# Four attention layers: the first layer's split weights stay on chip, and DMAs without inputs are tied to places in their queues

## Chip, cores, metric

One core of a Trainium2 chip runs the whole program. The metric is the device time of one execution in microseconds (us); the time before is the median of three runs. Engines are named as in the profile: PE (matrix products), PEld (its weight loads), DVE, ACT, POOL, and SP, which only issues DMAs.

## What is computed

Layers A, B, A, B with the same two sets of weights, on x of 2048 rows by 512 columns, with 32 heads of 16 columns:

```
x = x + A(layernorm(x));  x = x + B(layernorm(x));  x = x + A(layernorm(x));  x = x + B(layernorm(x))
qkv = x @ wqkv;  p = softmax(q @ k^T * 16 ** -0.5);  out = (p @ v) @ wo
A: query i sees keys j with 0 <= i - j < 256;   B: every query sees every key
```

## The kernel before, in words

**Tiles.** The 2048 rows are cut into four chunks c of 512. Within a sliding layer (0 and 2) the attention of a chunk runs over eight groups qd of four heads, and each group over three steps u; "step 0.3.1" below is chunk 0, group 3, u = 1. In a step PE makes scores s (L675) from tiles kt and qt, ACT takes their exponential into e (L679), POOL zeroes what the window excludes (affine_select, L742 and L745), and two steps later PE multiplies e with the values vt into acc (L752). The full layers (1 and 3) do the same with 16 steps and no mask (L719).

**Projections as side work.** The products K, Q, V of a chunk and the output product O of a finished chunk are cut into pieces of 4 to 20 matmuls (L387) and put between the steps of the attention. Lists per chunk (`side0` for layer 0) say which works are offered. A work starts when those it names as `deps` are done by a model clock kept in Python while the program is written; PE's order is fixed as written. The other engines' orders come from a scheduler, which moves an instruction forward when nothing that it knows of holds it. Each engine then runs its list in order, and an instruction that waits holds all behind it, DMA issues on SP and POOL included.

**Split weights.** Products are made from pairs of 16-bit halves. A weight of 512x512 is loaded raw in 32 bits (tile wr, 1 MB, `load_w`), ACT makes the high half and DVE the low half (tile w, L290 and L291, `parts`), and the pair is stored to DRAM (wd, 1 MB) and loaded again before each use (`weights`, L348). Weights are named `w<type>_<s>`: type 0 is A, 1 is B; s is 0 for q, 1 for k, 2 for v, 3 for o. Before the change w0_1, w0_0 and w0_2 serve two chunks from chip (`WT` holds two uses); for chunks 2 and 3 they come back from DRAM, and w0_3 always does. B's four weights are prepared (`PR`, `prep`) while chunk 0 and chunk 1 of layer 0 run.

**Operands in DRAM.** Keys and queries are stored by SP (kw, kf, qs; L508 to L512) and loaded per group: in layer 0 by POOL (`load_win`, L705 to L708), later by SP. One row block of these arrays is constant, and `fill` (L266 to L269) writes it from tiles of ones and zeros: two fills and the first qs on SP, the others on POOL.

**Ring of eight.** Each SP issue also waits until the SP DMA eight before it is done, and so does each POOL issue for POOL's. A chunk's x goes through norm on DVE (L426, L432) and a DMA transpose (L453, issued by SP, in set-up by ACT) into xc, the moving operand of K, Q and V. Tags name rings of buffers: "vf", "xc" and "vw" hold raw weights, split weights, xc and vt in turn.

Of the kernel before, what the change touches and what calls it, by code (L numbers as in the profile page):

```python
# [2 lines left out]

# [186 lines left out]
def fast_path(ctx, tc, flag, a_x, a_wqkv, a_wo, b_wqkv, b_wo, out):  # L190
# [21 lines left out]
    WT, ST, SP, pend = {}, {}, {}, []  # L212

    clock, DONE, XNR, ONR = [0.0], {}, {}, {}

    def spent(us):
        clock[0] += us
# [41 lines left out]

    def fill(t, key, c0=0, c1=1, q=nc.gpsimd):
        r4 = lambda d0, d1: rows(t).rearrange("h (d b) (c n) -> h d b c n", b=4, n=QC)[:, d0:d1, 3]
        for c in range(c0, c1):
            if key:
                q.dma_start(r4(0, 1)[:, 0, c], ones[:H])  # L266
                q.dma_start(r4(1, DH)[:, :, c], zeros[:H, None, :].broadcast_to([H, DH - 1, QC]))
            else:
                q.dma_start(r4(1, DH)[:, :, c], ones[:H, None, :].broadcast_to([H, DH - 1, QC]))  # L269


    def load_w(ty, s, tag="vf", n="wr", behind=None):
        raw = wp.tile([P, NC, D], F32, name=f"{n}{ty}_{s}", tag=tag, bufs=VB if tag == "vw" else NQ)
        if behind is not None:
            nc.vector.tensor_copy(raw[:, 0, :1], behind)
        if s < 3:
            nc.sync.dma_start(raw, mats[ty, s].rearrange("(k p) f -> p k f", p=P))
        else:

            for u in range(2):  # L280
                for h in range(4):
                    nc.sync.dma_start(raw[32 * h + DH * u:32 * h + DH * u + DH],
                                      mats[ty, s].rearrange("(k u h d) f -> u h d k f", u=2, h=4, d=DH)[u, h])
        return raw

    def parts(ty, s, raw):

        w = wp.tile([P, NC, 2, D], F16, name=f"w{ty}_{s}", tag="vf", bufs=NQ)
        for k in range(NC):
            nc.scalar.activation(w[:, k, 0, :], raw[:, k, :], AF.Copy, scale=UP[s])  # L290
# [170 lines left out]
    def project(l, s, c, act, ht=None, first=False):  # L461


        ty, n = l % 2, f"{l}_{s}_{c}" + ("" if ht is None else f"_h{ht}")
        here = n in WT or (ty, s) in WT
        w = weights(ty, s, n, *((0, D) if ht is None else (ht * P, (ht + 1) * P)))
        yield wait(0 if here else 8)
        xc = XC[l, c]
        if s == 0:
            dst = rows(qs[ty, c])  # L470
        elif ty == 0:
            dst = rows(kw[c])
        else:
            dst = rows(kf)[:, :, c * QC:(c + 1) * QC]
        sqs, begun = {}, []
        if first:
            for t in range(NHT):
                begun.append(bank())
                for k in range(NC):
                    nc.tensor.matmul(begun[t], w[:, k, 0, t * P:(t + 1) * P], xc[:, 0, k, :], start=(k == 0), stop=False)  # L480
                    spent(MM)
        for t in range(NHT) if ht is None else (ht,):
            w0 = t * P if ht is None else 0
            if first:
                ps = begun[t]
                yield from mms(ps, [(w[:, k, a, w0:w0 + P], xc[:, b, k, :]) for a, b in TERMS[1:] for k in range(NC)], go=False)
            else:
                ps = bank()
                yield from mms(ps, [(w[:, k, a, w0:w0 + P], xc[:, b, k, :]) for k in range(NC) for a, b in TERMS], 2.2)
            settle(not sqs)  # L490
            sp = vp.tile([P, 2, QC], F16, name=f"sp{n}_{t}", tag="sp", bufs=4)
            e = 1.0 / UP[s]
            with tc.high_priority(HEAD_START):
                if act:
                    nc.scalar.activation(sp[:, 0], ps, AF.Copy, scale=e)
                else:
                    nc.vector.tensor_scalar(sp[:, 0], ps, e, None, op0=ALU.mult)  # L497
                nc.vector.scalar_tensor_tensor(sp[:, 1], ps, e, sp[:, 0], op0=ALU.mult, op1=ALU.subtract)  # L498
            sq = vp.tile([P, QC], BF16, name=f"sq{n}_{t}", tag="sq", bufs=NHT)
            if act:  # L500
                nc.scalar.activation(sq, sp[:, 0], AF.Square)
            else:
                nc.gpsimd.tensor_tensor(sq, sp[:, 0], sp[:, 0], ALU.mult)  # L503
            sqs[t] = sq

            d = dst[8 * t:8 * t + 8].rearrange("h (d b) n -> (h d) b n", b=4)
            if s:
                nc.sync.dma_start(d[:, 0:2], sp[:, 0:1].broadcast_to([P, 2, QC]))  # L508
                nc.sync.dma_start(d[:, 2], sp[:, 1])
            else:  # L510
                nc.sync.dma_start(d[:, 0:2], sp)
                nc.sync.dma_start(d[:, 2], sp[:, 0])  # L512
            yield -MM if PH["full"] else -PH["run"] * MM
        return sqs

# [212 lines left out]
    def attn_win(l, c, qd, kt, qt, a):  # L728
        first = True
        for u, tiles in enumerate(WTILES):  # L730
            tiles = [p for p in tiles if c or p[0] >= 0]
            es_ = []
            for pr in range(2):
                e = exps(f"{l}_{c}_{qd}_{u}_{pr}", kt, qt, pr,
                         [(WIN + j * P, q * P, nb * P, s * P) for j, q, nb, s in tiles])
                ev = e.rearrange("p h (m n) -> p h m n", n=P)
                edges = [(s + b, q + b - j == 2) for j, q, nb, s in tiles for b in range(nb) if q + b - j != 1]
                for b, far in edges:
                    v = ev[:, :, b, :]
                    with tc.high_priority(HEAD_START):  # L740
                        if far:
                            nc.gpsimd.affine_select(v, v, pattern=[[0, 2], [-1, P]], compare_op=ALU.is_gt,  # L742
                                                    fill=0.0, base=0, channel_multiplier=1)
                        else:
                            nc.gpsimd.affine_select(v, v, pattern=[[0, 2], [1, P]], compare_op=ALU.is_ge,  # L745
                                                    fill=0.0, base=0, channel_multiplier=-1)
                es_.append(e)

            def pv(u=u, tiles=tiles, es_=es_):
# [160 lines left out]
    def run(g):  # L910
        for _ in g:
            pass

    def later(f, *a):

        yield from f(*a)
# [49 lines left out]
        return Work(later(lambda: transpose(l, c, XN.pop((l, c), ()))), 0.0, ("T", l, c), [("N", l, c)], aside=True)  # L966

    def K(l, c, act=True):
        return Work(later(keys, l, c, act), PK, ("K", l, c), [("T", l, c), ("P", l % 2, 1), ("P", l % 2, 0)], True)

    def Q(l, c, act=True, after=()):
        k = [("K", l, i) for i in (c - 1, c) if i >= 0] if l % 2 == 0 else list(after)
# [26 lines left out]
                    [("T", l, c), ("P", l % 2, 2), *after], True)  # L999

    def OO(l, c, tail=False):
        return Work(later(wo, l, c, tail), PO, ("N", l + 1, c), [("O", l, c, NHT - 1), ("P", l % 2, 3)], True)

    def NN(c, after=()):
        def gen():
            xs = load_x(0, c)
            yield wait(8)
            for i in range(4):
                stats(0, c, i, xs[i])
# [12 lines left out]
        return Work(prep(ty, s), 0.0, ("P", ty, s), after, aside=True)  # L1022

    def SW(ty, s, after):
        return Work(store(ty, s), 0.0, None, after, aside=True)

    def CM(ty, s, after=()):
        return Work(column_maxima(ty, s), 0.0, ("C", ty, s), after, aside=True)
# [9 lines left out]
    fill(kw[0], True, q=nc.sync)  # L1038
    fill(qs[0, 0], False, q=nc.sync)
    for i in range(4):  # L1040
        stats(0, 0, i, xs[i])
    mv = ST[0, 0][1]
# [35 lines left out]

    def side0(c):
        if c == 0:  # L1080
            return [F([(kw[1], True), (qs[0, 1], False), (kw[2], True), (qs[0, 2], False)]), SW(0, 1, [("K", 0, 1)]), NN(2), T(0, 2), Q(0, 1), SW(0, 0, [("Q", 0, 1)]), PR(0, 3, [("K", 0, 1)]), VV(0, 1), SW(0, 2, [("V", 0, 1, (0, 1), 0)]), PR(1, 1, [("V", 0, 1, (0, 1), 0)]), K(0, 2), NN(3, [("T", 0, 2)])]
        if c == 1:
            return [F([(kw[3], True), (qs[0, 3], False)]), T(0, 3), Q(0, 2), PR(1, 0, [("P", 0, 3)]), K(0, 3), VV(0, 2), PR(1, 2, [("P", 1, 1)]), OO(0, 0), T(1, 0), PR(1, 3, [("P", 1, 0)])]
        if c == 2:
            return [OO(0, 1), Q(0, 3), VV(0, 3), K(1, 0), T(1, 1)]
        return [F([(kf, True, k, k + 1) for k in range(NQ)] + [(qs[1, k], False) for k in range(NQ)]), K(1, 1), VV(1, 0, True, (0,)), OO(0, 2), Q(1, 0), T(1, 2), K(1, 2)]

    def side2(c):
        if c == 0:
# [89 lines left out]
```

## Time and profile before

| | us |
|---|---|
| median of three runs (lowest, highest) | 2721.22 (2715.78, 2726.24) |
| profiled execution, its own time | 2722.56 |
| its span, first to last instruction | 2720.6 |
| PE busy in the span | 2599.0 (96%) |
| ACT busy | 2376.8 (87%) |
| POOL busy, DMA issues not counted | 592.2 (22%) |

Read by stages: set-up until about 56 us, layer 0's attention from 68 to 422, a tail of projections until 482, the full layer 1, then layers 2 and 3. In the full layers ACT and PE are both over 95% busy; in layer 0 PE is nearly full and the others are not.

### The profile page before, as it was taken

Reading aid. Unit: us, or ns where it says so; the run is one execution under the profiler, and the core shown is the slowest. Engines: PE = TensorE matmul, PEld = TensorE weight load, DVE = VectorE, ACT = ScalarE, POOL = GpSimd, SP = SyncE. Lnnn points to the kernel's source line nnn. Section 1 sums busy time; section 2 is a strip of 40 time slices with the busy share of each in tenths; the row PEclk is TensorE's granted clock in tenths of the full one; section 3 lists DMA queues with packets and bytes.
Section 4 is the critical chain, followed back from the end, with each engine's and each line's share of the span. In section 5 each row is a group of like instructions: output and inputs, shape, how many; then the busy total and the mean of one; then the engine's idle time right before and its main releaser. Section 6 shows DMA issues by size and latency. Waiting matters only on the chain.

```text
span 2720.6 us, 59477 instructions
## 1 busy us (share of the span) xinstructions
PE 2599.0 (96%) x24315; PEld 751.6 (28%) x24315; DVE 859.3 (32%) x1949; ACT 2376.8 (87%) x2683; POOL 592.2 (22%) x1263
## 2 busy tenths in 40 slices
PE   7879999999999999999999999899999999999997
PEld 3233344222222222222223333422222222222221
DVE  6545654013243113111216576311222221121111
ACT  3665663999999999999997767499999999999997
POOL 2777771000000000000005688100000000000000
PEclk9999999999999999999999999999999999999999
DMA  9986766224343223212324665523343333333331
GB/s 283 277 263 203 187 197 206 77 91 124 117 118 104 64 82 109 84 64 92 100 73 148 194 168 168 158 80 103 105 121 124 124 107 111 98 108 119 97 95 49
DMA packets 300011, 353.14 MB, mean 130 GB/s; under 512 B 114432, under 2 KB 205024, under 8 KB 293712
## 3 DMA queue, kind: packets, MB, share of 16 engines
q1 hardware_dynamic: 286992, 321.16, 39.1%
q0 software_dynamic: 8512, 27.04, 3.6%
q8 instruction: 192, 3.15, 0.5%
q10 hardware_dynamic: 4224, 1.05, 0.2%
q14 instruction: 91, 0.75, 0.1%
HBM read 236.45 MB, written 96.99 MB: 123 GB/s over the span
## 4 chain that ended last, share of the span: by engine, by line
PE 77%; ACT 7%; DVE 6%; issue 4%; DMA 4%; SPq 1%; POOL 1%; ACTq 0%; DVEq 0%; POOLq 0%
PE acc L719 30%; PE s L675 20%; PE b L387 10%; PE acc L384 10%; ACT e L679 6%; PE acc L752 5%; DMA wr<-in_B_wqkv_dram 1%; PE bs L387 1%; DVE wa L321 1%; DVE ot L647 1%; DMA wr<-in_A_wqkv_dram 1%; DMA wo<-wd 1%; DVE xh L432 1%; DVE xn L426 0%; DMA w<-wd 0%
## 5 line engine op out<-in xcount | busy, mean ns | idle before, releaser
L679 ACT ACTIVATE e<-s 128x1024 f32<-128x1024 f32 (+2 forms) x2432 | 2245.6, 1112 | 152.1 <-PE s L675 126.6
L719 PE MATMUL acc<-e,vt 128*17 128x512 f32 x8192 | 1080.1, 599 | 5.0 <-DVE ot L647 4.0
L675 PE MATMUL s<-qt,kt 64*128 64x512 f16 (+3 forms) x5504 | 769.0, 355 | 44.8 <-ACT e L679 26.2
L675 PEld LDWEIGHTS <-kt 64*128 64x128 f16 x5504 | 198.1, 94 | 786.6 <-issue 764.1
L745 POOL TENSOR_SCALAR_AFFINE_SELECT e<-e 128x256 f32<-128x256 f32 x512 | 230.7, 459 | 76.5 <-ACT e L679 75.2
L719 PEld LDWEIGHTS acc<-e,vt 128*17 128x17 f32 x8192 | 136.3, 95 | 385.6 <-issue 353.3
L647 DVE STREAM_TRANSPOSE ot<-acc 128x512 f32<-128x512 f32 x128 | 91.5, 715 | 438.4 <-PE acc L719 334.7
L742 POOL TENSOR_SCALAR_AFFINE_SELECT e<-e 128x256 f32<-128x256 f32 x448 | 196.6, 445 | 56.1 <-ACT e L679 51.3
L752 PE MATMUL acc<-e,vt 128*17 128x384 f32 (+2 forms) x2816 | 196.1, 391 | 2.7 <-POOL e L742 2.7
L663 POOL TENSOR_TENSOR oh<-o,oh 128x512 f16<-128x512 f32 x31 | 36.0, 1161 | 716.9 <-DVE oh L662 653.7
L387 PE MATMUL b<-xc,w 128*128 128x512 f16 x676 | 164.7, 386 | 15.2 <-DVE sp L498 5.9
L604 POOL TENSOR_SCALAR vt<-vt 128x16 f32<-128x16 f32 (+1 forms) x96 | 24.2, 254 | 407.1 <-DVE vt L602 288.5
L503 POOL TENSOR_TENSOR sq_h<-sp_h 128x512 bf16<-128x512 f16 x27 | 28.1, 1041 | 388.9 <-DVE sp_h L497 388.9
L384 PE MATMUL acc<-xc,w 128*32 128x512 f16 x1344 | 108.9, 379 | 2.7 <-DMA xc<-xh 1.8
L384 PE MATMUL acc<-xc,w_h 128*32 128x512 f16 x1296 | 108.5, 379 | 2.3 <-DVE km L536 2.3
L387 PEld LDWEIGHTS <-w 128*128 128x128 f16 x800 | 72.5, 99 | 135.8 <-issue 57.7
L503 POOL TENSOR_TENSOR sq<-sp 128x512 bf16<-128x512 f16 x28 | 29.1, 1041 | 367.1 <-DVE sp L497 367.1
L497 DVE TENSOR_SCALAR sp_h<-acc 128x512 f16<-128x512 f32 x27 | 18.6, 690 | 282.4 <-PE acc L384 282.4
L635 DVE SCALAR_TENSOR_TENSOR x<-acc,x 128x512 f32<-128x512 f32 x60 | 41.5, 692 | 206.1 <-PE acc L384 200.1
L497 DVE TENSOR_SCALAR sp<-acc 128x512 f16<-128x512 f32 x28 | 19.3, 688 | 271.7 <-PE acc L384 271.7
L384 PE MATMUL acc<-wo,oh 128*32 128x512 f16 x1296 | 101.3, 379 | 3.3 <-DVE m_None L548 3.3
L602 DVE COPY vt<-acc 128x256 f32<-128x256 f32 (+1 forms) x36 | 18.5, 514 | 264.7 <-PE acc L384 264.7
(142 smaller groups left out, 1688.7 us busy)
## 6 DMA issues: line engine op xcount, KB each, us to landing
kt<-kf SPq DMA_DIRECT2D x128, 512.0 KB
xd<-x SPq DMA_DIRECT2D x96, 256.0 KB
x<-xd SPq DMA_DIRECT2D x96, 256.0 KB
qt<-qs SPq DMA_DIRECT2D x96, 256.0 KB
w<-wd SPq DMA_DIRECT2D x20, 1024.0 KB
qs<-sp SPq DMA_DIRECT2D x48, 256.0 KB
wo<-wd SPq DMA_DIRECT2D x12, 1024.0 KB
wv<-wd SPq DMA_DIRECT2D x17, 512.0 KB
```

The source lines that it names most:

```text
L384: nc.tensor.matmul(ps[g:g + 32], a[:, g:g + 32], b, start=(i == 0), stop=(i == len(pairs) - 1), skip_group_check=True)
L387: nc.tensor.matmul(ps, a, b, start=(go and i == 0), stop=(i == len(pairs) - 1))
L497: nc.vector.tensor_scalar(sp[:, 0], ps, e, None, op0=ALU.mult)
L503: nc.gpsimd.tensor_tensor(sq, sp[:, 0], sp[:, 0], ALU.mult)
L635: nc.vector.scalar_tensor_tensor(xs[i], ps, 1.0 / (UP[2] * UP[3]), xs[i], op0=ALU.mult, op1=ALU.add)
L647: nc.vector.transpose(ot.rearrange("p b r -> p (b r)"), a)
L675: nc.tensor.matmul(ps[:, h, s0:s0 + wd_], kt[R * h:R * h + R, pr, kc:kc + P], qt[R * h:R * h + R, pr, qc:qc + wd_], start=True, stop=True)
L679: nc.scalar.activation(e[:, :, w0:w1], ps[:, :, w0:w1], AF.Exp, scale=SCALE)
L719: nc.tensor.matmul(a[32 * h:32 * h + DH + 1, :], V[l, qd // 4, j // 8][:, j % 8, 4 * (qd % 4) + h, :], es_[h // 2][:, h % 2, :], start=(j ...
L742: nc.gpsimd.affine_select(v, v, pattern=[[0, 2], [-1, P]], compare_op=ALU.is_gt, fill=0.0, base=0, channel_multiplier=1)
L745: nc.gpsimd.affine_select(v, v, pattern=[[0, 2], [1, P]], compare_op=ALU.is_ge, fill=0.0, base=0, channel_multiplier=-1)
L752: nc.tensor.matmul(a[32 * h:32 * h + DH + 1, q * P:(q + nb) * P], V[l, (4 * c + j) // 4][:, j % 4, 4 * qd + h, :], es_[h // 2][:, h % 2, s ...
```

## The change

- `parts` keeps every A weight on chip: w0_0 to w0_2 for all four chunks, w0_3 for two. SP loses eight loads of 1 MB in layer 0 (four of w, two of wo, two of wv). No matmul is added or dropped.
- The stores of A's pairs to DRAM (`SW`) come later, after the last use in layer 0; w0_3 is stored through `SW` too.
- B's weights are prepared from chunk 1 on instead of from chunk 0 on, each after the store that frees its buffer; their raw tiles take buffers of "xc". PR(1,3) moves to chunk 3.
- Fills, raw loads, weight stores and the x loads of `NN` get `issue_after`: they are scheduled behind the last key or query store written so far (SP) or the last affine_select (POOL).
- The first two fills move behind K(0,0)'s stores; the lists of `side0` are reordered to use the weights while they are there.

```
+    def queued(e):
+        return tc.issue_after(LAST[e]) if e in LAST else nullcontext()
...
-        if ty == 0 and s < 3:
-            WT[ty, s] = [w, w]
+        if ty == 0:
+            WT[ty, s] = [w] * (NQ if s < 3 else 2)
             SP[ty, s] = w
...
     def store(ty, s):
-        nc.sync.dma_start(wd[ty, s], SP.pop((ty, s)))
+        with queued("SP"):
+            nc.sync.dma_start(wd[ty, s], SP.pop((ty, s)))
...
-        raw = load_w(ty, s)
+        raw = load_w(ty, s, "xc" if ty else "vw")
...
-                nc.sync.dma_start(d[:, 2], sp[:, 1])
+                last = nc.sync.dma_start(d[:, 2], sp[:, 1])
...
+            LAST["SP"] = last.ins
...
+                    LAST["POOL"] = last.ins
...
-        ... ("K", l, c), [("T", l, c), ("P", l % 2, 1), ("P", l % 2, 0)], True)
+        ... ("K", l, c), [("T", l, c), ("P", l % 2, 1)], True)
...
     xs = load_x(0, 1)
     run(keys(0, 0, True, None, True))
+    fill(kw[0], True, e="SP")
+    fill(qs[0, 0], False, e="SP")
```

The lists of `side0` by chunk, without the waits that the works name:

```
-  c0: F(kw1, qs1, kw2, qs2), SW(0,1), NN(2), T(0,2), Q(0,1), SW(0,0), PR(0,3), VV(0,1), SW(0,2), PR(1,1), K(0,2), NN(3)
+  c0: F(kw1, qs1, kw2, qs2), NN(2), T(0,2), Q(0,1), PR(0,3), VV(0,1), K(0,2), NN(3)
-  c1: F(kw3, qs3), T(0,3), Q(0,2), PR(1,0), K(0,3), VV(0,2), PR(1,2), OO(0,0), T(1,0), PR(1,3)
+  c1: F(kw3, qs3), T(0,3), SW(0,3), Q(0,2), VV(0,2), K(0,3), SW(0,1), PR(1,1), OO(0,0), T(1,0)
-  c2: OO(0,1), Q(0,3), VV(0,3), K(1,0), T(1,1)
+  c2: Q(0,3), SW(0,0), PR(1,0), VV(0,3), SW(0,2), PR(1,2), OO(0,1), K(1,0), T(1,1)
-  c3: F(kf, qs of B), K(1,1), VV(1,0), OO(0,2), Q(1,0), T(1,2), K(1,2)
+  c3: F(kf, qs of B), K(1,1), VV(1,0), OO(0,2), PR(1,3), Q(1,0), T(1,2), K(1,2)
```

From layer 1 on, PE and SP stand in the same order in both programs; all that moves lies before. Three places matter, with names that keep their numbers (`wr1_1` is the raw k weight of B, `e0_0_5_2_1` the exponential of layer 0, step 0.5.2, second pair).

SP, before the change, at chunk 0: a 1 MB store, two raw loads of B and a reload stand between the key stores of K(0,2).

```order
L300 DMA wd0_2_107<-w0_2_449 128x4096
L277 DMA wr1_1_1234<-in_B_wqkv_dram 128x4x512
L508 DMA kw2_94<-sp0_1_2_0_1310 128x2x512
L509 DMA kw2_94<-sp0_1_2_0_1310 128x512
L348 DMA w0_0_2_1627<-wd0_0_105 128x4096
L277 DMA wr1_0_1635<-in_B_wqkv_dram 128x4x512
L508 DMA kw2_94<-sp0_1_2_1_1411 128x2x512
```

SP after the change, first raw load of B, in chunk 1, behind K(0,3)'s last key store; below it the second and third, in chunk 2.

```order
L517 DMA kw3_95<-sp0_1_3_3_2417 128x2x512
L518 DMA kw3_95<-sp0_1_3_3_2417 128x512
L309 DMA wd0_1_106<-w0_1_203 128x4096
L285 DMA wr1_1_2458<-in_B_wqkv_dram 128x4x512
L628 DMA xd_113<-x0_0_2221 128x512
```

```order
L309 DMA wd0_0_105<-w0_0_303 128x4096
L520 DMA qs0_3_100<-sp0_0_3_3_3018 128x1024
L285 DMA wr1_0_3059<-in_B_wqkv_dram 128x4x512
L309 DMA wd0_2_107<-w0_2_449 128x4096
L564 DMA qs0_3_100<-m0_3_None_3134 8x512 x4
L285 DMA wr1_2_3653<-in_B_wqkv_dram 128x4x512
```

The raw loads leave chunk 0 and stand directly behind a 1 MB store each.

ACT, the split of wr1_1: before, in step 0.5.2.

```order
L679 ACTIVATE e0_0_5_2_1_1337<-s0_0_5_2_1_1332 128x1024
L290 ACTIVATE w1_1_1484<-wr1_1_1234 128x512 x4
L679 ACTIVATE e0_0_6_0_0_1382<-s0_0_6_0_0_1379 128x2x384
L679 ACTIVATE e0_0_6_0_1_1389<-s0_0_6_0_1_1386 128x2x384
L495 ACTIVATE sp0_1_2_1_1411<-b34_1317 128x512
```

And after the change, in step 1.6.2; the key stores ahead of its load are those of step 1.5.2.

```order
L689 ACTIVATE e0_1_6_2_0_2538<-s0_1_6_2_0_2533 128x1024
L689 ACTIVATE e0_1_6_2_1_2548<-s0_1_6_2_1_2543 128x1024
L298 ACTIVATE w1_1_2729<-wr1_1_2458 128x512 x4
L689 ACTIVATE e0_1_7_0_0_2583<-s0_1_7_0_0_2578 128x1024
L689 ACTIVATE e0_1_7_0_1_2593<-s0_1_7_0_1_2588 128x1024
```

The split still stands between exponentials, one chunk later.

POOL, the loads for group 4 of chunk 0: before, the key load stands in step 0.2.0, and a fill behind it.

```order
L706 DMA kt0_0_4_1023<-kw0_92 128x2x512
L745 AFFINE_SELECT e0_0_2_0_1_890<-e0_0_2_0_1_890 128x2x128
L742 AFFINE_SELECT e0_0_2_0_1_890<-e0_0_2_0_1_890 128x2x128
L266 DMA kf_96<-ones_85 32x512
L267 DMA kf_96<-zeros_89 32x15x512
```

After the change both loads stand behind the masks of step 0.3.1.

```order
L755 AFFINE_SELECT e0_0_3_1_0_1050<-e0_0_3_1_0_1050 128x2x128
L755 AFFINE_SELECT e0_0_3_1_1_1056<-e0_0_3_1_1_1056 128x2x128
L614 TENSOR_SCALAR vt0_1_0_0_923<-vt0_1_0_0_923 128x32
L715 DMA qt0_0_4_1022<-qs0_0_97 128x2x512
L716 DMA kt0_0_4_1021<-kw0_92 128x2x512
```

The load moved from six steps ahead of its first use, step 0.4.0, to two. The loads of group 5 stand likewise behind step 0.4.1, and those of group 6 in chunk 3 behind step 3.5.1 (before: behind 3.3.1 and 3.3.2).

More of the change, by code (lines that the diff above doesn't have):

```diff
@@ L1 @@
 from collections import deque
-from contextlib import ExitStack
+from contextlib import ExitStack, nullcontext
 import concourse.bass as bass
@@ L214, in fast_path @@
     clock, DONE, XNR, ONR = [0.0], {}, {}, {}
+    LAST = {}
+    def queued(e):
+        return tc.issue_after(LAST[e]) if e in LAST else nullcontext()
     def spent(us):
@@ L258, in fast_path, with fill @@
     nc.vector.memset(lsum, 0.0)
-    def fill(t, key, c0=0, c1=1, q=nc.gpsimd):
+    def fill(t, key, c0=0, c1=1, e="POOL"):
+        q = nc.gpsimd if e == "POOL" else nc.sync
         r4 = lambda d0, d1: rows(t).rearrange("h (d b) (c n) -> h d b c n", b=4, n=QC)[:, d0:d1, 3]
-        for c in range(c0, c1):
+        with queued(e):
+          for c in range(c0, c1):
             if key:
@@ L275, in load_w @@
             nc.vector.tensor_copy(raw[:, 0, :1], behind)
[L276 to L283, printed above, removed]
+        with queued("SP"):
+            if s < 3:
+                nc.sync.dma_start(raw, mats[ty, s].rearrange("(k p) f -> p k f", p=P))
+            else:
+                for u in range(2):
+                    for h in range(4):
+                        nc.sync.dma_start(raw[32 * h + DH * u:32 * h + DH * u + DH],
+                                          mats[ty, s].rearrange("(k u h d) f -> u h d k f", u=2, h=4, d=DH)[u, h])
         return raw
@@ L299, in store @@
     def store(ty, s):
-        nc.sync.dma_start(wd[ty, s], SP.pop((ty, s)))
+        with queued("SP"):
+            nc.sync.dma_start(wd[ty, s], SP.pop((ty, s)))
         yield 0.0
     def prep(ty, s):
-        raw = load_w(ty, s)
+        raw = load_w(ty, s, "xc" if ty else "vw")
         yield wait(20)
@@ L508, in project @@
                 nc.sync.dma_start(d[:, 0:2], sp[:, 0:1].broadcast_to([P, 2, QC]))
-                nc.sync.dma_start(d[:, 2], sp[:, 1])
+                last = nc.sync.dma_start(d[:, 2], sp[:, 1])
             else:
                 nc.sync.dma_start(d[:, 0:2], sp)
-                nc.sync.dma_start(d[:, 2], sp[:, 0])
+                last = nc.sync.dma_start(d[:, 2], sp[:, 0])
+            LAST["SP"] = last.ins
             yield -MM if PH["full"] else -PH["run"] * MM
@@ L968, in K @@
     def K(l, c, act=True):
-        return Work(later(keys, l, c, act), PK, ("K", l, c), [("T", l, c), ("P", l % 2, 1), ("P", l % 2, 0)], True)
+        return Work(later(keys, l, c, act), PK, ("K", l, c), [("T", l, c), ("P", l % 2, 1)], True)
     def Q(l, c, act=True, after=()):
@@ L1001, in OO @@
     def OO(l, c, tail=False):
-        return Work(later(wo, l, c, tail), PO, ("N", l + 1, c), [("O", l, c, NHT - 1), ("P", l % 2, 3)], True)
+        return Work(later(wo, l, c, tail), PO, ("N", l + 1, c), [("O", l, c, NHT - 1), ("P", l % 2, 3)] + [("S", 0, 3)] * (l == 0 and c > 1), True)
     def NN(c, after=()):
         def gen():
-            xs = load_x(0, c)
+            with queued("SP"):
+                xs = load_x(0, c)
             yield wait(8)
@@ L1024, in SW @@
     def SW(ty, s, after):
-        return Work(store(ty, s), 0.0, None, after, aside=True)
+        return Work(store(ty, s), 0.0, ("S", ty, s), after, aside=True)
     def CM(ty, s, after=()):
@@ L1037, in fast_path @@
     raw = {m: load_w(0, m, "xc") for m in (1, 0, 2)}
-    fill(kw[0], True, q=nc.sync)
-    fill(qs[0, 0], False, q=nc.sync)
     for i in range(4):
@@ L1080, in side0 @@
         if c == 0:
[L1081 removed]
+            return [F([(kw[1], True), (qs[0, 1], False), (kw[2], True), (qs[0, 2], False)]), NN(2), T(0, 2), Q(0, 1), PR(0, 3, [("K", 0, 1)]), VV(0, 1), K(0, 2), NN(3, [("T", 0, 2)])]
         if c == 1:
[L1083 removed]
+            return [F([(kw[3], True), (qs[0, 3], False)]), T(0, 3), SW(0, 3, [("P", 0, 3)]), Q(0, 2), VV(0, 2), K(0, 3), SW(0, 1, [("K", 0, 3)]), PR(1, 1, [("S", 0, 1)]), OO(0, 0), T(1, 0)]
         if c == 2:
[L1085 to L1086 removed]
+            return [Q(0, 3), SW(0, 0, [("Q", 0, 3)]), PR(1, 0, [("S", 0, 0)]), VV(0, 3), SW(0, 2, [("V", 0, 3, (0, 1), 0)]), PR(1, 2, [("S", 0, 2), ("P", 1, 0)]), OO(0, 1), K(1, 0), T(1, 1)]
+        return [F([(kf, True, k, k + 1) for k in range(NQ)] + [(qs[1, k], False) for k in range(NQ)]), K(1, 1), VV(1, 0, True, (0,)), OO(0, 2), PR(1, 3, [("P", 1, 2)]), Q(1, 0), T(1, 2), K(1, 2)]
     def side2(c):
```

4 lines of the change are left out of this document (2 added, 2 removed).

## The prediction, made before the changed kernel ran

> **What bounds the kernel now.** First the stages: busy time of each engine by stretch of the span, with granted PE clock, share of the DMA engines and GB/s in the last three columns.
>
> ```profile
> core 0: us, PE busy (x) PEld busy (x) DVE busy (x) ACT busy (x) POOL busy (x), PEclk, DMA share, GB/s
> 0.00:56.00 56.00, 36.70 (x169) 17.37 (x170) 37.10 (x89) 21.67 (x37) 12.75 (x31) 0.97 0.95 287
> 56.00:108.00 52.00, 51.31 (x366) 18.68 (x365) 30.41 (x73) 34.83 (x53) 35.02 (x76) 0.97 0.92 243
> 108.00:168.00 60.00, 37.27 (x319) 12.59 (x317) 36.18 (x83) 33.74 (x49) 39.28 (x78) 0.83 0.99 312
> 168.00:240.00 72.00, 71.09 (x653) 28.54 (x646) 31.55 (x73) 50.21 (x64) 56.69 (x129) 1.00 0.66 217
> 240.00:250.00 10.00, 5.51 (x36) 1.86 (x34) 9.41 (x26) 2.69 (x3) 5.74 (x14) 0.85 0.68 220
> 335.00:422.00 87.00, 85.28 (x810) 36.70 (x812) 46.78 (x110) 58.67 (x74) 64.72 (x148) 1.00 0.64 191
> 482.00:2720.00 2238.00, 2174.78 (x20883) 575.00 (x20879) 589.48 (x1332) 2098.83 (x2302) 306.88 (x626) 0.99 0.36 108
> ```
>
> From 482 on, 82% of the span, nothing that the change moves stands in PE's or SP's order, so I leave that part at its length and expect it to begin earlier or later as a block. In layer 0 PE sets the pace (71.1 of 72 us busy in 168 to 240) except in one stretch: from 108 to 168 it is idle for 60 - 37.3 = 22.7 us and runs at a clock of 0.83, with the DMA engines full (0.99). So layer 0 is PE work plus stalls, and the question is which stalls go. PE's waits up to 482, with total, times and longest:
>
> ```profile
> PE s L675 <- ACT e L679: 16.2, 8, 10.6
> PE b L387 <- DVE sp L498: 6.8, 4, 5.3
> PE acc L752 <- POOL e L742: 2.7, 2, 2.1
> PE b L387 <- issue: 2.3, 1, 2.3
> ```
>
> The first two lie almost all in chunk 0. Why, ACT and SP show in order of time (start, duration, and in brackets the idle time before and what ended it):
>
> ```profile
> 127.66 2.19 ACT L290 ACTIVATE w<-wr 128x512 f16<-128x512 f32 x4 [8.27 <-DMA wr<-in_B_wqkv_dram]
> 159.07 1.15 ACT L290 ACTIVATE w<-wr 128x512 f16<-128x512 f32 x2 [8.54 <-DMA wr<-in_B_wqkv_dram]
> ```
>
> ```profile
> 111.96 0.49 SPq L277 DMA_DIRECT2D wr<-in_B_wqkv_dram  x1
> 116.82 0.38 SPq L508 DMA_DIRECT2D kw<-sp  x1
> 126.61 0.34 SPq L509 DMA_DIRECT2D kw<-sp  x1
> ```
>
> ACT stands 8.3 and 8.5 us before a split of B's raw weights, with exponentials behind it; and between two halves of one key store SP stands 9.8 us, with the sp buffers that PE's next product needs. The chain of waits has the two loads (start, length):
>
> ```profile
> 111.96 15.67 DMA wr<-in_B_wqkv_dram
> 145.50 13.55 DMA wr<-in_B_wqkv_dram
> 240.89 5.95 DMA w<-wd
> ```
>
> A megabyte takes 14 to 16 us there and 6 us where the DMA share is 0.68.
>
> **What goes, in order of time.** Rows of PE around the other stalls, a usual row of four matmuls, and DVE's wait for x at the start:
>
> ```profile
> 55.82 4.47 PE L387 MATMUL bs<-xc,w 128*128 128x512 f16 x12 [5.35 <-DVE st L406]
> 60.12 2.75 PE L387 MATMUL b<-xc,w 128*128 128x512 f16 x12
> 126.63 1.87 PE L387 MATMUL b<-xc,w 128*128 128x512 f16 x4 [5.33 <-DVE sp L498]
> 161.18 0.61 PE L675 MATMUL s<-qt,kt 64*128 64x128 f16 x4 [10.59 <-ACT e L679]
> 246.88 3.46 PE L387 MATMUL b<-xc,w 128*128 128x512 f16 x8 [4.49 <-DMA w<-wd]
> 71.04 1.04 PE L387 MATMUL b<-xc,w 128*128 128x512 f16 x4
> ```
>
> ```profile
> 7.85 0.69 DVE L406 BATCH_NORM_STATS2 st<-x 128x6 f32<-128x512 f32 x1 [0.83 <-DMA x<-in_A_x_dram]
> ```
>
> (a) Start: six fills of POOL and three of SP no longer share the DMA engines with the first x tiles, whose last wait was 0.83 us: 1 us, between 0 and 1.6.
> (b) K(0,1) waits 5.35 us at 50.5 for transposed x, then runs its first twelve matmuls in 4.47 instead of 2.75 us. What is late is the four transposes on ACT's queue, issued under a DMA share of 0.95. They now come before the last evictions of Q(0,0), with 3 MB of fills and a 1 MB store less around them. 7.1 us go; ACT must wait in between for DVE's xh, which I put at 2 us on PE: 5 net, between 0 and 7.
> (c) K(0,2) waits 2.3 us at 108.6 for xc and a reload of w0_1; the reload and two stores ahead of it are gone: 2.3 (0 to 2.3).
> (d) The stretch 108 to 168: 22.7 - 2.3 = 20.4 us idle, and slow matmuls (four in 1.87 us where 1.04 is usual, and so on). A clock of 0.83 over 37.3 us of work bounds the latter at 6.3; I take 4. No raw load, no reload and one 1 MB store is left in chunk 0: 24 (12 to 26).
> (e) The reload of w0_0 for Q(0,3): 4.49, and eight matmuls in 3.46 where twice 1.04 is usual: 6 (4.5 to 6).
> (f) POOL's wait for chunk 3's queries, stored late, goes as Q(0,3) moves ahead of O: 2.7 (0 to 2.7).
> Sum: 1 + 5 + 2.3 + 24 + 6 + 2.7 = 41.
>
> **What comes.** (g) *Late key loads.* POOL in order of time, PE's scores, and the landing of POOL's loads (KB, median us):
>
> ```profile
> 97.26 0.79 POOL L705 DMA_DIRECT2D qt<-qs  x1
> 98.06 0.77 POOL L745 TENSOR_SCALAR_AFFINE_SELECT e<-e 128x256 f32<-128x256 f32 x2
> ```
>
> ```profile
> 101.12 0.56 PE L675 MATMUL s<-qt,kt 64*128 64x384 f16 x4
> 106.29 0.61 PE L675 MATMUL s<-qt,kt 64*128 64x384 f16 x8
> ```
>
> ```profile
> kt<-kw POOLq DMA_DIRECT2D x32, 256.0 KB, 4.5
> kw<-zeros POOLq DMA_DIRECT2D x3, 480.0 KB, 9.6
> ```
>
> The row at 98.06 is the two masks of step 0.3.1; without the load ahead of them they end at 98.0. Then qt and kt go out at 98.0 and 98.8, and kt lands 4.5 later, at 103.3, where the scores of 0.4.0 stood at 101.12: 2.2 us of wait. Group 5 stands behind the masks of 0.4.1, which end near 106; kt lands at 106 + 0.8 + 4.5 = 111.3, where 0.5.0 would follow the scores at 106.29 by some 2.5: 2.5 of wait. Group 6 of chunk 3 stands nearer its use too; with DMA engines at 0.64 there, a few tenths. I take 5 in all: between 0 (landings 2.5 us shorter) and 25 (these three and group 7 of chunk 3 land like the fills in 9.6, each 5.1 later: 5 + 4 x 5.1).
>
> (h) *Raw loads of B in chunks 1 and 2.* Side work of chunk 1 takes 3.4 to 4.2 us a step (starts of scores):
>
> ```profile
> 213.03 0.61 PE L675 MATMUL s<-qt,kt 64*128 64x256 f16 x8
> 217.25 0.61 PE L675 MATMUL s<-qt,kt 64*128 64x384 f16 x8
> 220.62 0.61 PE L675 MATMUL s<-qt,kt 64*128 64x128 f16 x8
> ```
>
> In the new order of ACT some ten exponentials' worth of time, three steps, lies between K(0,3)'s last matmul and the split of wr1_1: 4.2 + 3.7 + 2.4 = 10.3 us, of which 2.3 pass until SP issues the load, so 8.0 are left for the 1 MB store ahead of it and the load. 2 MB take 6.7 us at the 312 GB/s of the full stretch, or 2 x 5.95 = 11.9 by the reload of (e): a wait between 0 and 3.9. The other two (wr1_0 and wr1_2) stand the same way. I take 1 each, nearer the quick end since the share was 0.66 there before: 3, between 0 and 25 (three waits of the 8.3 to 8.5 of before).
>
> The Trainium skill, "DMA: Bandwidth & Descriptors", section "Queues, rings and completion order", has each DMA engine take a ring's descriptors in ring order, and one issuer's DMAs share a ring; so a raw load would begin only behind the store. The same page's table of measured sizes has 6.15 us for 1 MB, by which (h) were three times 4.3, 13 in place of 3. The reload's 5.95 agrees with that figure; that the store holds the load up no row of before shows.
>
> (i) *Steps without side work.* In the new order of PE six steps of chunk 0 and chunk 3 have no side work; before the change there were six too, but four of them lay at the stall of 108 that goes. PE then waits for ACT:
>
> ```profile
> 403.22 0.39 PE L675 MATMUL s<-qt,kt 64*128 64x256 f16 x4 [1.04 <-ACT e L679]
> ```
>
> Half of 1.04 at each: 3 (0 to 6).
>
> (j) *Twelve fills on POOL in chunk 3*, tied between masks. One issue, and POOL's waits in 330 to 422 (total, times, longest):
>
> ```profile
> 79.62 0.70 POOL L267 DMA_DIRECT2D kf<-zeros  x1
> ```
>
> ```profile
> POOL e L742 <- ACT e L679: 10.6, 13, 2.0
> POOL qt L705 <- PE s L675: 6.5, 5, 1.9
> ```
>
> 12 x 0.70 = 8.4 us go into 17.1 us of waits in these two rows; the masks are two steps ahead of PE's product. I take 2: 0 to 8.4.
>
> At nothing I put these. K no longer waits for q's preparation, and the two fills moved behind K(0,0) stand on SP ahead of nothing that PE uses before step 0.0.0; if they hold up the loads of group 0, that is three issues, 3 x 0.7 by POOL's row. Raw tiles of B use buffers of "xc", which are held until an earlier chunk's products are done; the load then waits in SP with the x loads behind it, and a free buffer is there since T(1,0) comes after. Uncovered, that is one step of 4.2. The three late stores of A's pairs are needed only in layer 2.
>
> Sum of costs: 5 + 3 + 3 + 2 = 13. **Net 41 - 13 = 28** from the profiled execution's 2722.6 gives 2694.6. That execution stands 1.3 above the median of the three, so the forecast is 2693.
>
> **Rivals.**
> *Late loads are slow loads (same).* If all four late key loads land in 9.6 us, (g) is 25: 28 - 20 = 8 gained, 2713. For it: fills and stores still share chunk 0's engines. Against it: 4.5 is the median under a full share. It decides from landings of about 7 us.
> *ACT behind queued raw loads (slower).* Place: the three splits of wr1_1, wr1_0 and wr1_2. Each load is issued directly behind a 1 MB store. If both run at the pace of the stretch 108 to 168, the load lands 2 x 15.67 = 31.3 us after the pair's issue; with 8.0 us of cover ACT waits 23.3, three times 70, and PE's exponentials stand behind it. 70 in place of 3 is 67 more: 28 - 67 = -39, about 2760. The net turns negative once each of the three waits exceeds (28 + 3) / 3 = 10.3 us, a landing 18.3 after the issue. For it: the order puts a store ahead of each load, and ACT waited 8.3 and 8.5 before. Against it: the DMA share in 168 to 240 and 335 to 422 is 0.66 and 0.64, and eight other megabytes have gone.
> *The change does not empty the engines.* A share of 0.99 in 108 to 168 may be owed to x loads, transposes and key stores, which all stay; then half of (d) remains: 28 - 12 = 16, 2705.
>
> **How the numbers follow.** Forecast 0.62, 2676 to 2707; late loads 0.14; ACT behind raw loads 0.15; engines not emptied 0.09. The low end is all gains at their upper bounds (1.6 + 7 + 2.3 + 26 + 6 + 2.7 = 45.6) with no cost, 2722.6 - 45.6 = 2677, less the 1.3; the high end of the forecast has (g) to (j) twice as large. The range reaches to 2730: that takes in the late loads, the engines not emptied, and waits behind raw loads of up to 13 us each (31 - 39 = -8); that rival at its own price is left out. Half a per cent, 13.6 us, is about what a measurement of this kernel can tell from no change, so "same" is 2707.6 to 2734.8. Faster is the forecast and half of the engines not emptied: 0.67; slower is the raw-load rival: 0.15; same is the rest, 0.18.
>
> **What the changed profile would show.** (b) the wait of PE at the start of K(0,1) under 2 us; (d) the stretch 108 to 168 with over 55 us of PE busy and a clock near 1.00, and no ACT row waiting for wr in chunk 0; (e) no PE wait on w from wd before 300; (g) PE's scores waiting for kt on POOL's loads, 2 us twice; (h) ACT's splits of B in chunks 1 and 2 with idle time ahead under 2 us; (j) no second product of PE waiting long for masks in chunk 3. The block behind 482 keeps its 2238 us. It would be wrong if that block grew, if the raw loads' waits in (h) exceeded 10 us, or if PE in chunk 0 stayed idle for a reason other than these DMAs.

## The result, and the profile after

The changed kernel takes 2717.99 us (median of 12 runs, 2710.82 to 2722.34) where the kernel before takes 2720.36 beside it (12 runs): a ratio of 0.9987, 95% interval 0.9975 to 0.9999. The forecast was 2693, a gain of 28; the gain is 2.4. In profiled executions it is 1.0 us (2722.56 to 2721.54). Single runs of one kernel lie up to 12 us apart, so sums of profiled waits below are good to a few us, and ratios carry the verdicts; they leave out a few executions at a granted clock of 0.65 to 0.85, which took 2916 us or more.

The stages of the changed kernel, in the columns and stretches of the table before:

```profile
0.00:56.00 56.00, 38.19 (x172) 18.05 (x173) 35.07 (x87) 21.86 (x37) 6.82 (x20) 0.94 0.77 203
56.00:108.00 52.00, 48.17 (x358) 17.63 (x357) 30.59 (x73) 33.92 (x53) 31.31 (x70) 1.00 0.78 204
108.00:168.00 60.00, 54.92 (x487) 19.74 (x486) 38.36 (x91) 42.05 (x56) 52.68 (x111) 0.97 0.77 223
335.00:422.00 87.00, 74.71 (x692) 33.89 (x689) 45.61 (x105) 48.01 (x63) 53.96 (x122) 0.94 0.81 224
482.00:2720.00 2238.00, 2174.64 (x20863) 576.62 (x20859) 589.23 (x1332) 2093.98 (x2297) 306.70 (x626) 0.99 0.36 108
```

The stretch 108 to 168 did what was forecast: PE is busy 54.9 us instead of 37.3, at a clock of 0.97 instead of 0.83. But the stretch 335 to 422, where chunk 3 stands before the change, lost much of what chunk 0 won: 74.7 us busy where it was 85.3, with the DMA share up from 0.64 to 0.81. PE's waits up to 482, with total, times and longest:

```profile
PE s L685 <- DMA kt<-kw: 16.1, 6, 4.7
PE b L396 <- DVE sp L507: 9.0, 5, 3.3
PE bs L530 <- ACT sq L510: 6.9, 1, 6.9
PE s L685 <- ACT e L689: 6.4, 10, 1.1
```

The wait for ACT's exponentials has fallen from 16.2 to 6.4, and two waits are new: 16.1 us for keys and 6.9 for an eviction at the start.

Where the lead goes is read from a mark that both programs have 128 times: DVE's transpose of a finished group of heads. Here are those of group 2 of chunk 0, group 4 of chunk 1, the last groups of chunks 2 and 3, layer 1's first group and the program's last group, of before:

```profile
97.14 0.72 DVE L647 STREAM_TRANSPOSE ot<-acc 128x512 f32<-128x512 f32 x1 [1.05 <-PE acc L752]
214.69 0.72 DVE L647 STREAM_TRANSPOSE ot<-acc 128x512 f32<-128x512 f32 x1 [4.03 <-PE acc L752]
338.10 0.72 DVE L647 STREAM_TRANSPOSE ot<-acc 128x512 f32<-128x512 f32 x1 [0.83 <-PE acc L752]
423.73 0.72 DVE L647 STREAM_TRANSPOSE ot<-acc 128x512 f32<-128x512 f32 x1 [0.56 <-PE acc L752]
515.88 0.72 DVE L647 STREAM_TRANSPOSE ot<-acc 128x512 f32<-128x512 f32 x1 [3.19 <-PE acc L719]
2706.16 0.72 DVE L647 STREAM_TRANSPOSE ot<-acc 128x512 f32<-128x512 f32 x1 [10.68 <-PE acc L719]
```

And of the changed kernel:

```profile
97.01 0.72 DVE L657 STREAM_TRANSPOSE ot<-acc 128x512 f32<-128x512 f32 x1 [0.89 <-PE acc L763]
195.02 0.72 DVE L657 STREAM_TRANSPOSE ot<-acc 128x512 f32<-128x512 f32 x1 [3.60 <-PE acc L763]
316.28 0.72 DVE L657 STREAM_TRANSPOSE ot<-acc 128x512 f32<-128x512 f32 x1 [3.12 <-PE acc L763]
418.50 0.72 DVE L657 STREAM_TRANSPOSE ot<-acc 128x512 f32<-128x512 f32 x1 [0.56 <-PE acc L763]
510.90 0.72 DVE L657 STREAM_TRANSPOSE ot<-acc 128x512 f32<-128x512 f32 x1 [3.19 <-PE acc L729]
2702.94 0.72 DVE L657 STREAM_TRANSPOSE ot<-acc 128x512 f32<-128x512 f32 x1 [10.68 <-PE acc L729]
```

The differences are the lead: 0.1, 19.7, 21.8, 5.2, 5.0 and 3.2 us. Chunk 3 alone takes back 16.6. (A mark stands behind a group of heads, not behind a fixed amount of projection work; where the two programs differ in that, it is said below.) The next experiments ask why, and whether the start and the ties matter; the "lead" in them is always this difference to the kernel before.

### The profile page after: what moved, and what is told of

It is laid out like the page before. It is cut to its first block, busy times and chain, and to the rows that moved or that the text cites. A ratio compares the mean times of both kernels' runs of the same rounds, so it can differ in the third digit from the quotient of the medians.

```text
span 2719.8 us, 59481 instructions
## 1 busy us (share of the span) xinstructions
PE 2602.8 (96%) x24315; PEld 754.1 (28%) x24315; DVE 859.0 (32%) x1949; ACT 2378.3 (87%) x2683; POOL 588.2 (22%) x1263
## 4 chain that ended last, share of the span: by engine, by line
PE 75%; DVE 8%; ACT 7%; issue 4%; DMA 4%; POOL 1%; SPq 0%; ACTq 0%; DVEq 0%; POOLq 0%
PE acc L729 30%; PE s L685 20%; PE acc L393 10%; PE b L396 9%; ACT e L689 6%; PE acc L763 4%; PE bs L396 1%; DMA kt<-kw 1%; DVE ot L657 1%; DVE wa L330 1%; DVE xh L441 1%; DMA wr<-in_B_wqkv_dram 1%; DVE xn L435 1%; DMA wo<-wd 1%; DVE xh L435 0%
## 5 line engine op out<-in xcount | busy, mean ns | idle before, releaser
L685 PE MATMUL s<-qt,kt 64*128 64x512 f16 (+3 forms) x5504 | 771.0, 356 | 49.9 <-DMA kt<-kw 16.1
```

Source lines behind the costliest of these rows:

```text
L685: nc.tensor.matmul(ps[:, h, s0:s0 + wd_], kt[R * h:R * h + R, pr, kc:kc + P], qt[R * h:R * h + R, pr, qc:qc + wd_], start=True, stop=True)
```

## Experiments

All ratios are to the kernel before, run beside; the changed kernel's own is 0.9987.

**Fills of B away from chunk 3, to the end of layer 0** (bfills_tail).

```
-  c3: F(kf, qs of B), K(1,1), VV(1,0), OO(0,2), PR(1,3), Q(1,0), T(1,2), K(1,2)
+  c3: K(1,1), VV(1,0), OO(0,2), PR(1,3), Q(1,0), T(1,2), K(1,2), F(kf, qs of B) once Q(1,0) is done
```

> The changed kernel with the twelve fills of B's arrays (kf, qs of layer 1) moved behind Q(1,0), to the end of layer 0; nothing else moved. Theory: chunk 3 gives back 16.6 us (the lead falls from 21.8 us at the end of chunk 2 to 5.2 at the end of chunk 3) because these fills push POOL's key loads one to three steps back; PE waits 11.8 us for kt there. Then the waits for kt in chunk 3 vanish, the lead at the end of chunk 3 is 19 to 22 us, and the time is 12 to 16 us below the changed kernel, about 2703, unless layer 1 waits longer for kf at its start (2.6 us now). Rival: what crowds chunk 3 is the raw output weight of B (eight loads), its store and the x stores; the key loads stay late, PE still waits 8 us or more for kt in chunk 3, and the time stays within 4 us of 2718.

Measured: 2722.36 us, 0.9994 (0.9980 to 1.0008). PE's waits from chunk 3 to the start of layer 1:

```profile
PE b L396 <- DMA wo<-wd: 5.1, 1, 5.1
PE s L685 <- DMA kt<-kf: 3.9, 1, 3.9
PE s L685 <- ACT e L689: 3.4, 6, 1.0
PE b L396 <- DVE sp L507: 2.8, 1, 2.8
```

No wait for kt from kw is left in chunk 3, so the fills did cause it, as the theory said and the rival denied. Yet the time did not fall. The lead is 13.3 us at the end of chunk 3 and 5.8 at the end of layer 1's first group: the fills now run beside the load of the output weight, which lands in 12.2 us (7.3 in the changed kernel). PE waits 5.1 us for it, and the first twelve matmuls behind it take 5.13 us where 2.76 is usual. The theory's time was wrong because it took the end of layer 0 for free ground.

**The key loads ahead of the fills** (loads_first). The fills stay in chunk 3; only POOL's order changes.

```
-        q.dma_start(qt, qs[0, c]...); q.dma_start(kt..., kw[c]...); if c: q.dma_start(kt..., kw[c - 1]...)
+        with tc.high_priority(HEAD_START) if l == 0 else nullcontext():
+            q.dma_start(qt, qs[0, c]...); q.dma_start(kt..., kw[c]...); if c: q.dma_start(kt..., kw[c - 1]...)
```

> The changed kernel with POOL's key and query loads of layer 0 given priority in the scheduler; the fills stay in chunk 3. In chunk 0 the key loads of groups 4 and 5 go out two to three steps earlier, in chunk 3 those of groups 3, 5, 6 and 7 half a step to two steps earlier. Theory that the place of the load decides: the two waits of chunk 0 (4.4 us) go and of the 11.8 us in chunk 3 some 5 to 8 go: 9 to 12 us below the changed kernel, about 2707. Rival that the fills' traffic decides (a key load took 5.3 to 7.6 us to land in chunk 3, 4.5 before): the waits in chunk 0 go, those in chunk 3 stay above 8 us, and the time falls by 3 to 5 us, about 2714.

Measured: 2709.45 us, 0.9946 (0.9929 to 0.9963), that is 0.41% or 11 us below the changed kernel. Landing times of POOL's loads in chunk 3 (KB, median us), before the change, after it, and here:

```profile
kt<-kw POOLq DMA_DIRECT2D x5, 256.0 KB, 3.3
```

```profile
kt<-kw POOLq DMA_DIRECT2D x4, 256.0 KB, 6.3
```

```profile
kt<-kw POOLq DMA_DIRECT2D x4, 256.0 KB, 6.0
```

In the stretch of these rows, 338 to 424, the loads land about as slowly as in the changed kernel; over the whole of chunk 3 the median is 5.0 instead of 6.1 us. PE waits for no kt from kw in the whole layer, since the loads go out earlier: an earlier place in POOL's order is a cure. That does not make the slow landing harmless. The four loads that PE waited for in the changed kernel, second halves of 128 KB, took 5.3 to 7.6 us. At 3.8, their median before the change, the four waits would come to 1.4 us instead of 11.8, an estimate from the two traces.

**The four transposes of set-up on SP** (tr_sp).

```
-        transposed(0, 1, i, xh, nc.scalar)
+        transposed(0, 1, i, xh)
```

> The changed kernel with the four transposes of chunk 1's normalised x in set-up issued by SP in place of ACT. Theory: ACT's wait at these transposes holds the evictions of Q(0,0), which is PE's 6.9 us wait at 39; it goes, the first scores of step 0.0.0 start 4 to 6 us before 65.8, and the time falls by 4 to 6 us, about 2713. Rival: the transposes now hold SP, with the query stores of Q(0,0) behind them, so the first query loads of POOL (at 54 now) or the transposed x itself are late and the first scores start within 2 us of 65.8: no gain beyond 2 us.

Measured: 2712.90 us, 0.9962 (0.9944 to 0.9980), 0.25% or 7 us below the changed kernel. In the changed kernel ACT's rows of the start read:

```profile
36.46 5.09 ACTq L462 DMA_TRANSPOSE xc<-xh  x1
41.67 0.60 ACT L504 ACTIVATE sp<-bs 128x512 f16<-128x512 f32 x1 [4.61 <-issue]
41.69 3.55 ACTq L462 DMA_TRANSPOSE xc<-xh  x1
45.29 0.63 ACT L510 ACTIVATE sq<-sp 128x512 bf16<-128x512 f16 x1 [3.02 <-issue]
```

These two transposes occupy ACT's queue for 5.1 and 3.6 us, with evictions of Q(0,0) behind them, and PE waits for the last one. In the second of them ACT is not waiting for its input: DVE writes the last xh by 37.6, and this transpose, the fourth, starts at 41.7 and still takes 3.6 us.

```profile
36.92 0.69 DVE L441 TENSOR_TENSOR xh<-xn,xh 128x512 f16<-128x512 f32 x1
```

On SP the wait is gone, and the first scores stand at 58.0:

```profile
57.98 0.50 PE L685 MATMUL s<-qt,kt 64*128 64x384 f16 x4
```

They stood at 65.80 in the changed kernel. The rival, that SP would be held instead, does not show.

**No fill tied** (fills_free).

```
-        with queued(e):
+        with nullcontext():
```

> The changed kernel with no fill tied: POOL's fills go back to the front of its list and into chunk 0, B's twelve included, and the key loads of chunk 3 go back to their places of before. The raw loads, stores and kept weights stay as changed. Theory: chunk 3's 16 us come back and chunk 0 pays 5 to 8 us for 8 MB of fills, so the time is 8 to 11 us below the changed kernel, about 2708; the stretch 108 to 168 keeps over 50 us of PE busy. Rival: the fills' absence from chunk 0, not that of raw loads and reloads, is what gave the 25 us there; then PE is busy under 45 us in that stretch and the time is above 2718.

Measured: 2709.23 us, 0.9947 (0.9930 to 0.9964), 0.40% or 11 us below the changed kernel. The stretch 108 to 168 and chunk 3:

```profile
108.00:168.00 60.00, 56.15 (x512) 20.72 (x504) 42.71 (x97) 43.27 (x57) 54.35 (x116) 1.00 0.80 236
335.00:422.00 87.00, 82.45 (x737) 39.38 (x736) 51.81 (x114) 46.99 (x63) 47.63 (x113) 1.00 0.68 198
```

With all fills back at the front and in chunk 0, PE is as busy there as in the changed kernel. From mark to mark chunk 3 takes back 5.7 us of the lead instead of 16.6. With the raw loads and reloads gone, chunk 0 does not need the fills to go as well: the ties of the fills cost 11 us and buy nothing. The theory's time came true, its terms did not: chunk 3 gives back 10.9 us and not 16, and chunk 0 does not pay 5 to 8, since the lead at group 4 of chunk 1 is 21.3 us, above the changed kernel's 19.7.

**The tie on POOL alone, in the kernel before** (before_tied; `queued` and the place of the last mask are as in the change).

```
+        with queued("POOL") if q is nc.gpsimd else nullcontext():
         for c in range(c0, c1):
```

> The kernel before the change with POOL's fills tied behind the last mask written, as in the change, and nothing else. Theory: the tie alone costs: key loads of chunk 3 move back by one to four steps (groups 4 to 7) and PE waits 8 to 16 us for kt there; chunk 0 gains at most 5 us at the start and in the stretch 108 to 168 stays below 42 us of PE busy; 4 to 10 us slower than the kernel before, ratio 1.0015 to 1.004. Rival: the fills were what filled the DMA engines in chunk 0; PE's busy time in 108 to 168 rises by 8 us or more and the ratio is 0.998 or less.

Measured: 2731.12 us, 1.0031 (1.0016 to 1.0045): slower, as the theory said. Chunk 3's waits:

```profile
PE s L681 <- DMA kt<-kw: 13.4, 4, 6.6
```

Here the place alone is enough. The key loads of the last two groups, issued at 391.6 and 407.3, land in 4.6 and 5.0 us, and PE waits 5.7 and 6.6 us for them.

But the theory's chunk 0 was too low: PE is busy 49.0 us in 108 to 168, not under 42, and the lead is 11.3 us at the end of chunk 2 before chunk 3 takes it and 5.6 more. So here, with the raw loads still there, taking the fills out of chunk 0 does help.

**B's preparation moved, nothing else** (raw_late, then raw_late_tied).

```
-  c0: ... PR(1,1), ...   c1: ... PR(1,0), ... PR(1,2), ... PR(1,3)
+  c1: ... K(0,3), VV(0,2), PR(1,1), ...   c2: ... Q(0,3), PR(1,0), VV(0,3), PR(1,2), ...   c3: ... PR(1,3), ...
```

> The kernel before the change with one part of the change alone: the preparation of B's four weights moves from chunks 0 and 1 to chunks 1, 2 and 3. Fills stay at the front, A's weights are stored and loaded again as before. Theory: ACT's waits for the raw loads (8.3 and 8.5 us) and the key store held behind one are most of the idle time in the stretch 108 to 168, so this part alone gives 12 to 17 of the 24 us there and the time falls by 10 to 15 us against the kernel before (ratio 0.9945 to 0.996). Rival: the reloads and stores of A's weights, which stay, fill the DMA engines as well; the stretch keeps under 47 us of PE busy and the ratio stays above 0.998.

Measured: 2731.98 us, 1.0039 (1.0025 to 1.0054). The move did not happen, as SP's rows show:

```profile
138.61 0.57 SPq L277 DMA_DIRECT2D wr<-in_B_wqkv_dram  x1
142.32 0.61 SPq L277 DMA_DIRECT2D wr<-in_B_wqkv_dram  x1
152.00 1.63 SPq L277 DMA_DIRECT2D wr<-in_B_wqkv_dram  x1
```

A load without inputs goes wherever its buffer comes free in the scheduler's order, whatever list names it: all three are still in chunk 0 (before the change at 112, 128 and 146 us). Neither theory is tested by it. The second try adds the tie (`queued` as in the change):

```
+        with queued("SP") if ty else nullcontext():
```

> The kernel before the change with B's preparation moved to chunks 1 to 3 and its raw loads tied behind the last key or query store on SP, as in the change; fills, stores and reloads of A's weights stay. (In the try without the tie the scheduler had put the raw loads back into chunk 0, at 138 to 152 us.) Theory: ACT's two waits of 8 us in chunk 0 vanish, PE is busy 48 us or more in 108 to 168 and the ratio to the kernel before is 0.994 to 0.997. Rival: stores and reloads of A's weights alone keep the DMA engines full; PE's busy time there stays below 45 us and the ratio is 0.998 or above.

Measured: 2726.55 us, 1.0017 (1.0004 to 1.0030). In chunk 0 the theory holds: PE is busy 51.4 us in 108 to 168, and the lead is 13.5 us at the first group of chunk 1. Then chunk 2 takes it all. PE and ACT there:

```profile
234.80 0.61 PE L393 MATMUL b<-xc,w 128*128 128x512 f16 x1 [5.85 <-DMA w<-wd]
292.48 0.62 PE L527 MATMUL b<-sq,hsum 128*32 128x512 bf16 x4 [8.56 <-ACT vt L607]
```

```profile
291.31 0.63 ACT L296 ACTIVATE w<-wr 128x512 f16<-128x512 f32 x1 [9.28 <-DMA wr<-in_B_wqkv_dram]
```

The reload wait stays, and ACT waits 9.3 us for a raw load tied late, with an eviction behind it. So the time is the rival's (0.998 or above), but not for the rival's reason. Moving the raw loads pays only as long as no one needs them at once.

**No tie at all, weights kept** (untied).

```
-        return tc.issue_after(LAST[e]) if e in LAST else nullcontext()
+        return nullcontext()
```

> The changed kernel without any tie, on POOL or SP: A's weights stay on chip, but the scheduler puts their four stores and the first raw load of B, 5 MB, ahead of the key stores of K(0,2), and the fills at the front. Theory: SP's queue then holds K(0,2) as before the change; PE is busy under 48 us in 108 to 168 and the time is 0.998 to 1.004 of the kernel before, so the tie on SP is what the gain in chunk 0 hangs on. Rival: leaving out eight reloads is enough; PE is busy 53 us or more there and the ratio is 0.994 to 0.996, as with ties on SP alone.

Measured: 2712.45 us, 0.9958 (0.9943 to 0.9973).

```profile
108.00:168.00 60.00, 52.92 (x475) 19.20 (x474) 38.18 (x86) 40.70 (x54) 48.48 (x104) 0.97 0.82 250
```

That is the rival's time and, within 0.1 us, its busy share: chunk 0 runs even with three stores and a raw load ahead of K(0,2)'s key stores and a fourth store between them. The theory that the gain hangs on SP's tie falls. But the reloads are not all that is gone: two of the three raw loads that stood in chunk 0 before the change stand at 231 and 243 us here, without a tie, so no run leaves out the reloads alone. Against fills_free, which keeps SP's other ties (0.9947), the intervals overlap.

**Both repairs together** (trsp_free: transposes on SP, no fill tied; trsp_loads: transposes on SP, key loads first).

> The changed kernel with SP issuing the four transposes of set-up and with no fill tied, together. If the two gains lie in different places (start; chunks 0 and 3) they add: 0.25% and 0.40% below the changed kernel's 0.9987, so a ratio of 0.992 to 0.9925 to the kernel before, about 2700. Rival: a lead won before the projections at the end of layer 0 is taken back there by loads of weights that do not start earlier; then it stays at 0.9945 or above.

Measured: 2702.40 us, 0.9924 (0.9907 to 0.9941): the gains add.

> The changed kernel with SP issuing the four transposes of set-up, and with POOL's key and query loads of layer 0 given priority, the fills staying tied. By the same sum as for the kernel without ties: 0.25% and 0.41% below 0.9987, so 0.992, about 2700, with no wait of PE for kt above 1 us in layer 0. Rival: with an earlier start the loads of chunk 3 come into the fills' traffic and PE waits for kt again by 4 us or more; then 0.9945 or above.

Measured: 2701.85 us, 0.9918 (0.9901 to 0.9935), the lowest found, about 22 us below the kernel before, though its interval overlaps that of trsp_free. Its waits are read from a second run:

> The kernel with transposes on SP and loads first once more, for a profile at the usual clock. If the place of the key loads decides, PE waits for kt under 1 us in all of layer 0 and layer 1's first group ends 20 to 24 us before that of the kernel before; if the earlier start brings the loads into the fills' traffic, PE waits for kt by 4 us or more in chunk 3.

Measured: 2699.46 us beside 2723.64, one run each. PE's largest waits up to 482, apart from the first for x:

```profile
PE b L396 <- DVE sp L507: 11.5, 7, 3.3
PE s L685 <- ACT e L689: 7.3, 11, 1.0
PE s L685 <- DMA kt<-kf: 3.1, 1, 3.1
```

No wait for kt from kw is among them. The first group of layer 1 ends at 488.0, 27.9 us ahead of before, which is more than the 20 to 24 expected. The largest wait left is for sp, which DVE writes.

## Why the prediction was wrong, point by point

Most of the gain that is missing was lost in chunk 3, 16.6 us where 2 to 4 were priced, and at the start, 5.9 of 6.

**The block from 482 on** was taken to keep its length. Its lead goes from 5.0 to 3.2 us over 2190 us, and to 0.8 at the last instruction, where the last matmuls run slower (three in 1.48 us where 0.81 is usual). That is within the spread of single runs.

**(a) and (b), the start: 6 forecast, 2.2 measured at the first scores (67.99 to 65.80), and 0.1 by group 2.** K(0,1)'s wait of 5.35 us went, as forecast. The step that failed is the 2 us put on ACT's wait for DVE's xh at the transposes: PE waits 6.9 us there, and what holds ACT at last is a transpose whose input is ready (tr_sp). The rest went in two waits of PE for sp in chunk 0 (1.54 and 1.19 us): SP issues the eight raw loads of w0_3 in one piece ahead of Q(0,1)'s first store, 7.3 us after its tile was ready (70.4); that this held the later tiles was not tried.

```profile
69.97 7.29 SPq L290 DMA_DIRECT2D wr<-in_A_wo_dram  x8
77.68 0.34 SPq L520 DMA_DIRECT2D qs<-sp  x1
```

**(c) and (d), the stretch to 168: 26.3 forecast.** The lead grows by 19.5 from group 2 of chunk 0 to group 4 of chunk 1, with 4.4 us of waits for keys in between, so some 24. This was right in size, but the parts do not add. With the raw loads out and the reloads in (raw_late_tied) the lead at group 4 of chunk 1 is 13.3 us; with the reloads and two raw loads out (untied) it is 20.6. The fills count in chunk 0 beside raw loads (before_tied) and not without them (fills_free).

**(e), (f) and (h), the rest of chunks 1 and 2: 5.7 forecast net, 2.1 measured.** Even these 2.1 are no gain: twelve matmuls of projections, 2.3 us, stand in chunk 3 now instead. No reload is waited for, the wait of (f) has fallen from 2.7 to 0.3 us, and ACT's waits for raw loads are 1.26 and 2.31 us where 1 each was taken:

```profile
202.44 9.17 DMA wr<-in_B_wqkv_dram
246.12 9.55 DMA wr<-in_B_wqkv_dram
```

A raw load behind a 1 MB store lands in 9.2 to 9.6 us, so the rival that ACT would stand behind such loads did not come. The Trainium skill's page "DMA: Bandwidth & Descriptors" has ring order (section "Queues, rings and completion order") and 6.15 us for a megabyte (section "Bandwidth"), from which the prediction estimated 12.3 us for the pair. Counted from the store's issue the load landed after 9.7 and 10.6 us, so that estimate was high here. What was missing in the forecast is three waits of PE for sp, 1.89, 1.10 and 3.31 us, in the steps beside K(0,3) and K(1,0). That DVE is late there because splits, norm and evictions crowd on it was not tried.

**(i), steps without side work: 3 forecast, none measured.** PE's waits for exponentials in layer 0, other than the one of 10.6, were 5.6 us and are 4.7.

**(g) and (j), the late loads: this step failed.** For chunk 0 it stands: 2.2 and 2.5 us forecast, 0.92 and 3.46 measured. For chunk 3 the prediction had "a few tenths" for group 6 and 2 us for the fills, and the lead fell by 16.6. The four waits for kt are these:

```profile
349.35 1.04 PE L685 MATMUL s<-qt,kt 64*128 64x128 f16 x8 [3.23 <-DMA kt<-kw]
374.59 0.71 PE L685 MATMUL s<-qt,kt 64*128 64x128 f16 x6 [4.69 <-DMA kt<-kw]
388.71 0.61 PE L685 MATMUL s<-qt,kt 64*128 64x128 f16 x8 [1.69 <-DMA kt<-kw]
400.91 0.61 PE L685 MATMUL s<-qt,kt 64*128 64x128 f16 x8 [2.15 <-DMA kt<-kw]
```

That is 11.8 us for groups 3, 5, 6 and 7, and slow matmuls behind them (eight in 1.04 where 0.61 is usual). From mark to mark, the 16.6 us are 10.9 of more idle time (12.6 instead of 1.7), the 2.3 of moved matmuls, and 3.3 of slow ones: PE is busy 89.6 us with the work that takes 86.2 in fills_free, where the clock is 1.00.

Two things were overlooked. The fills were priced as POOL's issue time (8.4 us into 17.1 of waits), while what they moved was the order behind them: four groups' loads, not one. And the landing was priced at 4.5, which the prediction calls the median under a full share; it is the median over all of layer 0, and the eight loads of 56 to 168 had 5.2. In chunk 3 the fills (4 MB), the raw output weight and its store (1 MB each) raise what is moved from 16 to 22 MB and the landing from 3.3 to 6.3 us; without fills there (fills_free) the landing is 3.8.

Of the rivals, "late loads are slow loads" (2713, with a chance of 0.14 and a price of 20) came nearest to what happened. It had half of the cause: slow landings. The other half is the place: the fills also put back the loads of groups 3 and 5 of chunk 3, which the prediction does not name. loads_first shows that an earlier place ends the waits, and before_tied that a late place makes them even at landings of 4.6 and 5.0 us.

## What to carry to other kernels

A transfer that is taken out of a full stretch and tied elsewhere is paid again by what stands behind its new place: price the orders of the loads it pushes back, not only its issue. Look at the queue of the engine that issues it, and at who waits there two steps later. And where several transfers fill a stretch together, taking out some of them may end most of the stall, so that removing the rest as well brings little: here keeping the weights, with no tie at all, brought 0.42%, and the changed kernel with all its ties 0.13%.

## What the runs showed that was not expected

The DMA transposes of set-up occupy the queue that issues them: 1.7, 2.3, 5.1 and 3.6 us for the four on ACT, 8.1 us for the same four on SP. The fourth one's 3.6 us on ACT hold no wait for its input, which was ready 4 us before; for the others the runs do not tell how much is waiting for DVE's xh. Twelve fills of constants at the end of layer 0 were slow among themselves: the four of 480 KB for the queries, issued in 2.6 us, had a median of 13.6 us to landing, against 7.1 when they stood one by one between masks.
